# Top-32 attention and a gated mixture: seven column parts, a bound used in place, and another mask on GpSimd

## The chip, the cores and the metric

The kernel runs on one core of a Trainium2 chip. Its time is the device time of one execution in microseconds (us). The kernel before took 844.89 us, the median of three runs (844.6 to 846.16).

## What is computed

Eight batches with eight heads each, 576 tokens, 64 values a head. For every row of scores only the 32 largest count:

```python
scores = scale * np.matmul(q, k.transpose(0, 1, 3, 2))
kth = np.partition(scores, -top_k, axis=-1)[..., -top_k:-top_k + 1]
scores = np.where(scores >= kth, scores, -1000000000.0)
attn = softmax(scores)          # over the row
x = attn @ v                    # heads side by side: 8 x 576 x 512
```

Then, in each batch, the 128 tokens with the largest `x @ w_gate` get `sigmoid(gate) * relu(x @ w1) @ w2` added (w1 is 512 x 1024). This document calls that the mixture.

## The kernel before, in words

**Units.** The attention is cut into 144 units, 18 a batch. A unit holds two rows of heads for 128 queries: a tile `sc` of 128 partitions x 2 heads x 576 scores. The loop at line 1083 goes over n; in one turn it works on several units at once, each at another stage. Every instruction is recorded by the helper at line 43 and kept in program order on its engine, so the order of the code is the order of each queue; the trace shows nearly all instructions under L43, and they are told apart by their tiles.

**The stages of a unit**, by engine:

1. TensorE multiplies the scores (`multiply`, line 352); ScalarE copies them from PSUM to `sc` (`keep`, 369). This is done one turn ahead.
2. VectorE looks for a bound near the 24th largest (`find_bound`, 383). MAX8 gives the eight largest of each of eight parts of 72 columns. Three rounds of MAX8 on the candidates (the best 3, 7, 8 of each part), with MATCH_REPLACE8 between, give `best[2]`, whose eighth value is the bound.
3. One turn later ScalarE (`cut`, 413) casts the upper half of the bound's float32 to `seen`, then takes Sign of bound less score (`part`, 420), with the sum of the signs, which counts how many scores lie above. GpSimd multiplies score and sign (`y`) and appends eight filling values that depend on the count (`fill`, 435).
4. Another turn later VectorE takes the eight largest of `y`'s 584 columns (`find_kth`, 444): the eighth is the 32nd largest of the row.
5. Another turn later the mask `less` is made (`mask`, 449): of the unit's two heads, ScalarE makes one, as Relu(32nd - score), and GpSimd the other, as the comparison score < 32nd, 1 or 0. In the 9 units where GpSimd is not used, VectorE makes it.
6. Another turn later TensorE transposes the scores in 128 x 128 pieces (`turn_some`, 476) and adds `less` times a diagonal matrix of -2^90 (`out_of_reach`) into the same PSUM piece. Eight pieces lie in the tile `ptr`. The ninth, the last 64 columns of one head beside those of the other, lies in `av` (`turn_last`, 498). ScalarE then takes the exponential (`pT`, `last`), TensorE multiplies with `v` (`values`, 510), and ScalarE copies the result to `xs`.

**Other work in the turns.** `weigh` (1043) is followed by the next unit's mask, the scores of unit n+1, none, one or two transposes of the next batch's rows (`loads_at`), the products of `values`, and one step of an earlier batch's mixture (`mix_at`: products with w1 and w2). The first mixture step on TensorE falls some 33 units in. In the first units of each batch there are turns with no row transposes or no mixture step.

**The end.** After the last unit the last batch's mixture runs by itself. A set of checks (`seen`, `sums`, ranks) is reduced on VectorE to one number; if it says that a row's count was outside what the method can handle, a general path (`general`, 1315) computes everything again.

**What orders TensorE's array.** The products have different shapes: 128 rows x 128 columns for transposes and mask products, 64 x 128 for the scores (64 values a head), 128 x 64 for the products with v.

Of the kernel before, what the change touches and what calls it, by code (L numbers as in the profile page):

```python
# [11 lines left out]
ALU = mybir.AluOpType  # L12
FP32 = mybir.dt.float32
BF16 = mybir.dt.bfloat16
I32 = mybir.dt.int32
# [6 lines left out]
BIG = 2.0**90  # L22
# [4 lines left out]
LEAST = 1.0e-16 * SMALLER  # L27
# [2 lines left out]


J = 4


class InOrder:
# [11 lines left out]
def kernel(  # L47
# [28 lines left out]
    const = ctx.enter_context(tc.tile_pool(name="const", bufs=1))  # L76
# [3 lines left out]
    wkpool = ctx.enter_context(tc.tile_pool(name="wk", bufs=2))  # L80
    stats = ctx.enter_context(tc.tile_pool(name="stats", bufs=6))
# [38 lines left out]
    nc.vector.tensor_copy(out=slot, in_=slot_i)  # L120


    out_of_reach = const.tile([P, P], BF16, name="out_of_reach")
    nc.vector.tensor_scalar_mul(out_of_reach, ident, -BIG)

    NS = B * 2 * (J * NHP + NHP // 2)
    seen = const.tile([P, 3, NS], FP32, name="seen")  # L130
    sums = const.tile([P, B * NT, H], FP32, name="sums")
    nc.gpsimd.memset(sums, 1.0)

    MIDDLE = S - 2 * (TOP_K - 8) + 1
# [30 lines left out]
    def load_weights():  # L165
# [169 lines left out]
    def groups(t):  # L335

        return NHP // 2 if t == J else NHP
# [42 lines left out]
            )  # L380
        return sc

    def find_bound(sc):

        w = S // 8
        cand = wkpool.tile([P, 2, 64], FP32, name="cand")
        best = [stats.tile([P, 2, 8], FP32, name=f"best{r}") for r in range(3)]  # L390
        for i in range(2):

            if i == 1:
                flush_vector()
            for u in range(8):
                dve.max(cand[:, i, 8 * u : 8 * u + 8], sc[:, i, u * w : (u + 1) * w])


        parts = cand.rearrange("p i (u e) -> p i u e", u=8)
# [11 lines left out]
        return best[2]  # L411

    def cut(best, at):

        act.copy(
            out=seen[:, 0, at : at + 2],
            in_=best.rearrange("p i e -> p (i e)").bitcast(BF16)[:, 15:32:16],
        )

    def part(i, sc, at, sides):  # L420

        act.activation(
            sides[:, i, :],
            sc[:, i, :],
            AF.Sign,
            bias=seen[:, 0, at + i : at + i + 1],  # L430
            scale=-(1.0 + 2.0**-23),
            accum_out=seen[:, 2, at + i : at + i + 1],
        )

    def fill(y, at):

        pool.tensor_tensor(
            y[:, :, S : S + 8],
            steps,
            seen[:, 2, at : at + 2].unsqueeze(2).to_broadcast([P, 2, 8]),  # L440
            ALU.subtract,
        )

# [5 lines left out]
    def mask(sc, next8, on=None):  # L449

        less = wkpool.tile([P, 2, S], BF16, name="less")
        for i, engine in enumerate(on or (act, pool)):
            kth = next8[:, i, 7:8]
            if engine is act:
                act.activation(less[:, i, :], sc[:, i, :], AF.Relu, bias=kth, scale=-1.0)
            else:

                def is_less(engine=engine, i=i, kth=kth):
                    (engine or dve).tensor_scalar(
                        out=less[:, i, :],
                        in0=sc[:, i, :],
                        scalar1=kth,
                        scalar2=None,
                        op0=ALU.is_lt,
                    )

                if engine:  # L470
                    is_less()
                else:
                    vector_late.insert(0, is_less)
        return less

    def turn_some(tr, z, less):

        pe.transpose(tr, z, ident)
        if less is not None:
            pe.matmul(  # L480
                tr, less, out_of_reach, start=False, stop=True, skip_group_check=True
            )

    def room_to_turn():
        return ps_tr.tile([P, 2, J, P], FP32, name="ptr"), ps_av.tile(
# [3 lines left out]
    def turn(z, tr, less=None):  # L489

        for i in range(2):
            for c in range(J):
                at = slice(c * P + i * R, (c + 1) * P + i * R)
                turn_some(
                    tr[:, i, c, :], z[:, i, at], None if less is None else less[:, i, at]
                )

    def turn_last(z, av, less=None):

        tr = av[:, 512 - P : 512]
        last = [
            a and a.rearrange("p i s -> p (i s)")[:, JP : JP + P] for a in (z, less)
        ]
        turn_some(tr, *last)
        return tr

    def values(t, g, pT, last, av, vs):  # L510
# [475 lines left out]
    per_batch = sum(groups(t) for t in range(NT))  # L986
# [27 lines left out]
    for b in range(B - 1):  # L1014
        n = (b + 1) * per_batch + mix_at_of.get(b, mix_at)[6]
# [11 lines left out]
    def warm_up():  # L1027
        ps = ps_av.tile([P, 512], FP32, name="av")
        for _ in range(48):
            pe.matmul(ps[:, 0:P], out_of_reach, out_of_reach)  # L1030

    warm_up()
    turn_pair(first_rows, 0, dve.tensor_copy)
# [1 line left out]
    loading = iter(())  # L1035
    inverting = normalised = None
    of_batch = {}
    scs, bests, ys, next8s, masks = {}, {}, {}, {}, {}

    def is_unit(n):  # L1040
        return 0 <= n < N
# [1 line left out]
    def weigh(sc, tr, av, less):  # L1043
# [9 lines left out]

        return pT, last, exp

    def what_is_below(n):
        at, sc = 2 * n, scs[n]
        cut(bests.pop(n), at)
        sides = wkpool.tile([P, 2, S], BF16, name="sides")
        y = wkpool.tile([P, 2, S + 8], FP32, name="y")  # L1060
        for i in range(2):
            part(i, sc, at, sides)
            pool.tensor_tensor(y[:, i, 0:S], sc[:, i, :], sides[:, i, :], ALU.mult)
        fill(y, at)
        ys[n] = y

    def kth_of(n):
# [2 lines left out]
            next8s[b] = stats.tile([P, per_batch, 2, 8], FP32, name="next8", bufs=2)  # L1070
        find_kth(ys.pop(n), next8s[b][:, i, :, :])

    def mask_of(n, on=None):
        b, i = divmod(n, per_batch)
        masks[n] = mask(scs[n], next8s[b][:, i, :, :], on)
        if i == per_batch - 1:
            at = 2 * per_batch * b
            pool.tensor_copy(
                out=seen[:, 1, at : at + 2 * per_batch].rearrange("p (n i) -> p n i", i=2),
                in_=next8s.pop(b)[:, :, :, 7],  # L1080
            )

    for n in range(-1, N):
        b, i = divmod(n, per_batch)
# [63 lines left out]


        if is_unit(n):  # L1150
            bests[n] = find_bound(scs[n])
        flush_vector()
        flush_pool()
        if is_unit(n - 2):
# [8 lines left out]
        if gating is not None:  # L1163
            b, t = gating
# [5 lines left out]
        b, i = divmod(n, per_batch)  # L1170
# [69 lines left out]
    next(closed)  # L1240


    sure = stats.tile([P, 1], FP32, name="sure")
    dve.memset(sure, 1.0)
    for what, op, than, limit in (
        (seen[:, 0, :], ALU.min, ALU.is_gt, LEAST),
        (seen[:, 1, :], ALU.min, ALU.is_gt, LEAST),
        (seen[:, 2, :], ALU.max, ALU.is_lt, float(MIDDLE)),
        (seen[:, 2, :], ALU.min, ALU.is_gt, float(MIDDLE - 16)),
        (sums.rearrange("p t h -> p (t h)"), ALU.min, ALU.is_gt, FEWEST),  # L1250
        (sums.rearrange("p t h -> p (t h)"), ALU.max, ALU.is_lt, MOST),
    ):
# [138 lines left out]
```

## Time and profile before

| | us |
|---|---|
| median of 3 runs | 844.89 |
| profiled execution | 845.82 |
| its span, first to last instruction | 844.0 |
| TensorE (PE) busy | 793.1 |
| VectorE (DVE) busy | 805.4 |
| ScalarE (ACT) busy | 759.5 |
| GpSimd (POOL) busy | 729.6 |

A group's line in the profile has the engine, the operation, the tile written and those read, the shape out and in, the number of instructions, their busy time in us, the mean duration of one in ns, and the idle time ahead of them with what ended it. PE is TensorE's products, PEld its weight loads. An engine's next instruction may begin before the one ahead has ended, so the cost of one in a row of equals is the distance between starts, which is less than its duration. TensorE's ends are modelled. The granted TensorE clock was 0.992 on average.

### The profile page before, as it was taken

What the parts mean: (1) busy time and instruction counts of PE and PEld (TensorE: products, weight loads), DVE (VectorE), ACT (ScalarE), POOL (GpSimd) and SP (SyncE); (2) the same over time, 40 slices, a digit from 0 to 9 for tenths busy, and PEclk for the clock granted to TensorE, in tenths of its full rate; (3) what the DMA queues carried; (4) which work ended last, traced back from release to release, by engine and by line L of the source; (5) the groups of instructions that cost most, each with busy time, mean ns of one, the idle gap of its engine ahead of it and who ended that gap; (6) DMA issues with size and microseconds to landing.
All of it is one profiled execution on the core that took longest, in us unless ns stands there. A gap on an engine that the chain in (4) does not pass through costs nothing. (4 is left out here: it accounts for less than half of the span.)

```text
span 844.0 us, 28167 instructions
## 1 busy us (share of the span) xinstructions
PE 793.1 (94%) x9887; PEld 612.4 (73%) x9887; DVE 805.4 (95%) x4905; ACT 759.5 (90%) x1701; POOL 729.6 (86%) x730
## 2 busy tenths in 40 slices
PE   6898888998999999999999999999999999999987
PEld 5666666666787778877787777877788777867754
DVE  7899999999999999999999999999999999999960
ACT  4799999999999999999999999999999999979831
POOL 3689889989989899999999999999999999989831
PEclk9699999999999999999999999999999999999999
DMA  8931111411141221511323221412215102101021
GB/s 171 279 75 29 40 64 26 104 45 35 58 97 28 52 40 58 110 40 27 89 37 82 51 47 56 101 30 52 39 58 110 27 2 76 23 2 27 2 70 30
DMA packets 122134, 50.38 MB, mean 60 GB/s; under 512 B 116416, under 2 KB 116416, under 8 KB 120960
## 3 DMA queue, kind: packets, MB, share of 16 engines
q1 hardware_dynamic: 118672, 43.91, 21.6%
q0 software_dynamic: 1728, 4.20, 2.8%
q8 instruction: 80, 1.31, 0.7%
q14 instruction: 70, 0.57, 0.3%
q10 hardware_dynamic: 1584, 0.39, 0.2%
HBM read 36.93 MB, written 11.55 MB: 57 GB/s over the span
## 5 line engine op out<-in xcount | busy, mean ns | idle before, releaser
L43 POOL TENSOR_TENSOR y<-sc,sides 128x576 f32<-128x576 f32 x288 | 365.0, 1288 | 73.1 <-ACT sides L43 70.0
L43 DVE MAX8 cand<-sc 128x8 f32<-128x72 f32 x2304 | 330.9, 218 | 1.7 <-ACT sc L43 1.7
L43 POOL TENSOR_SCALAR less<-sc,next 128x576 bf16<-128x576 f32 x135 | 232.9, 1725 | 3.2 <-DVE next L43 2.5
L43 ACT ACTIVATE sides<-sc,seen 128x576 bf16<-128x576 f32 x288 | 221.0, 768 | 5.2
L43 PE MATMUL ptr<-out_of_reach,less 128*128 128x128 bf16 x1136 | 204.8, 220 | 16.2 <-POOL less L43 16.0
L43 PE MATMUL ptr<-ident,sc 128*128 128x128 f32 x1136 | 214.4, 279 | 0.0
L43 DVE MAX8 next<-y 128x8 f32<-128x584 f32 x288 | 204.4, 751 | 3.2 <-POOL y L43 3.2
L43 PE MATMUL ps<-kT,qT 64*128 64x288 f32 (+1 forms) x1280 | 180.9, 431 | 7.6 <-ACT qT L43 5.8
L43 PEld LDWEIGHTS av<-v,pT 128*64 128x64 f32 x4544 | 144.1, 137 | 46.3 <-ACT last L43 33.7
L43 PEld LDWEIGHTS ptr<-ident,sc 128*128 128x128 f32 x1136 | 160.8, 142 | 22.4 <-PE av L43 8.7
L43 PE MATMUL av<-v,pT 128*64 128x65 f32 x4544 | 163.7, 224 | 13.8 <-ACT last L43 12.2
L43 ACT COPY sc<-ps 128x1152 f32<-128x1152 f32 (+1 forms) x144 | 160.5, 1114 | 8.5 <-PE ps L43 7.2
L43 ACT ACTIVATE pT<-ptr 128x1024 f32<-128x1024 f32 x142 | 144.1, 1015 | 18.1 <-PE ptr L43 14.6
L43 PEld LDWEIGHTS <-less 128*128 128x128 bf16 x1296 | 133.2, 104 | 36.4 <-POOL less L43 21.8
L43 DVE MAX8 best<-cand 128x8 f32<-128x24 f32 (+2 forms) x864 | 142.4, 201 | 0.1
L43 PEld LDWEIGHTS ps<-kT,qT 64*128 64x128 f32 (+1 forms) x1280 | 97.8, 177 | 46.6 <-issue 22.1
L43 ACT ACTIVATE less<-sc,next 128x576 bf16<-128x576 f32 x143 | 110.6, 774 | 6.5 <-DVE next L43 6.3
L43 DVE MATCH_REPLACE8 cand<-best,cand 128x24 f32<-128x24 f32 (+1 forms) x576 | 101.9, 185 | 0.0
L43 PE MATMUL av<-vpair,last 128*128 128x130 f32 (+1 forms) x314 | 68.1, 317 | 0.0
L43 PE MATMUL h_ps<-xeT,w 128*128 128x128 f32 x464 | 61.6, 277 | 0.0
L43 PEld LDWEIGHTS h_ps<-xeT,w 128*128 128x128 f32 x464 | 56.0, 192 | 2.1 <-issue 1.2
L43 PE MATMUL y_ps<-w,hT 128*128 128x512 f32 x112 | 56.7, 601 | 0.0
(129 smaller groups left out, 869.7 us busy)
## 6 DMA issues: line engine op xcount, KB each, us to landing
v<-in_v_dram SPq DMA_DIRECT2D x64, 128.0 KB, 3.3
out_dram<-x SPq DMA_DIRECT2D x8, 1024.0 KB, 4.1
rows<-in_k_dram SPq DMA_DIRECT2D x56, 128.0 KB, 2.9
rows<-in_q_dram SPq DMA_DIRECT2D x56, 128.0 KB, 3.1
w<-in_moe_w_dram SPq DMA_DIRECT2D x2, 2048.0 KB
gate_row<-row_dram SPq DMA_DIRECT2D x7, 288.0 KB, 5.1
w<-in_k_dram SPq DMA_DIRECT2D x8, 128.0 KB, 3.4
last<-in_k_dram SPq DMA_DIRECT2D x8, 128.0 KB, 3.5
```

The lines of the kernel that those rows point to most:

```text
L43: return lambda *a, **kw: self._tc.keep_in_program_order(fn(*a, **kw))
```

## The change

It does four things.

1. `find_bound` cuts the 576 columns into 7 parts of 82 or 83 and not 8 of 72.
2. The bound is used in place: the third round writes into a tile `bound` that holds a batch's bounds, and Sign reads it there. `cut` and its cast are gone. What the checks need of the bounds and of the 32nd values is reduced on VectorE once a batch (`keep_least`, new), and no longer copied to `seen` (by GpSimd once a batch, for the 32nd).
3. GpSimd's mask (and VectorE's, where it stands in) for the unit's second head is min(score - 32nd, 0). It is at most 0, so it is multiplied by +2^90; `out_of_reach` becomes two matrices.
4. The ninth mask product holds columns of both heads, which now need different signs: it becomes two products of 64 columns each.

```diff
-    def find_bound(sc):
-        w = S // 8
-        cand = wkpool.tile([P, 2, 64], FP32, name="cand")
-        best = [stats.tile([P, 2, 8], FP32, name=f"best{r}") for r in range(3)]
+    def find_bound(sc, bound):
+        cand = wkpool.tile([P, 2, 8 * PARTS], FP32, name="cand")
+        best = [stats.tile([P, 2, 8], FP32, name=f"best{r}") for r in range(2)]
+        best.append(bound)
...
-            for u in range(8):
-                dve.max(cand[:, i, 8 * u : 8 * u + 8], sc[:, i, u * w : (u + 1) * w])
+            for u in range(PARTS):
+                dve.max(
+                    cand[:, i, 8 * u : 8 * u + 8],
+                    sc[:, i, u * S // PARTS : (u + 1) * S // PARTS],
+                )
...
-    def cut(best, at):
-        act.copy(
-            out=seen[:, 0, at : at + 2],
-            in_=best.rearrange("p i e -> p (i e)").bitcast(BF16)[:, 15:32:16],
-        )
...
-            bias=seen[:, 0, at + i : at + i + 1],
+            bias=bound[:, i, 7:8],
...
                         scalar1=kth,
-                        scalar2=None,
-                        op0=ALU.is_lt,
+                        scalar2=0.0 if i else None,
+                        op0=ALU.subtract if i else ALU.is_lt,
+                        **(dict(op1=ALU.min) if i else {}),
...
-    def turn_some(tr, z, less):
+    def turn_some(tr, z, less, heads):
         pe.transpose(tr, z, ident)
         if less is not None:
-            pe.matmul(
-                tr, less, out_of_reach, start=False, stop=True, skip_group_check=True
-            )
+            n = P // len(heads)
+            for u, i in enumerate(heads):
+                pe.matmul(
+                    tr[u * n : (u + 1) * n],
+                    less[:, u * n : (u + 1) * n],
+                    out_of_reach[i],
+                    start=False,
+                    stop=True,
+                    skip_group_check=True,
+                )
...
+    def keep_least(b, bound, kth):
+        low = stats.tile([P, per_batch, 2], I32, name="low", bufs=1)
+        dve.tensor_scalar(
+            out=low,
+            in0=bound.bitcast(I32),
+            scalar1=(1 << 23) - 1,
+            scalar2=1,
+            op0=ALU.bitwise_and,
+            op1=ALU.bitwise_xor,
+        )
+        for w, of in enumerate((bound, kth, low)):
+            dve.tensor_reduce(
+                out=least[:, w, b : b + 1], in_=of, axis=mybir.AxisListType.XY, op=ALU.min
+            )
```

`turn` passes one head to `turn_some`, `turn_last` both. The last batch's `keep_least` stands among the checks at the end, which read `least` (three reductions of 8) in place of two of `seen`'s 288 columns.

More of the change, by code (lines that the diff above doesn't have):

```diff
@@ L32 @@
 J = 4
+PARTS = 7
 class InOrder:
@@ L120 @@
     nc.vector.tensor_copy(out=slot, in_=slot_i)
-    out_of_reach = const.tile([P, P], BF16, name="out_of_reach")
-    nc.vector.tensor_scalar_mul(out_of_reach, ident, -BIG)
+    out_of_reach = [const.tile([P, P], BF16, name=f"out_of_reach{i}") for i in range(2)]
+    for i in range(2):
+        nc.vector.tensor_scalar_mul(out_of_reach[i], ident, BIG if i else -BIG)
     NS = B * 2 * (J * NHP + NHP // 2)
-    seen = const.tile([P, 3, NS], FP32, name="seen")
+    seen = const.tile([P, NS], FP32, name="seen")
+    least = const.tile([P, 3, B], FP32, name="least")
     sums = const.tile([P, B * NT, H], FP32, name="sums")
@@ L394, in find_bound @@
                 flush_vector()
-            for u in range(8):
-                dve.max(cand[:, i, 8 * u : 8 * u + 8], sc[:, i, u * w : (u + 1) * w])
-        parts = cand.rearrange("p i (u e) -> p i u e", u=8)
+            for u in range(PARTS):
[3 more added lines that the diff above has]
+                )
+        parts = cand.rearrange("p i (u e) -> p i u e", u=PARTS)
         for r, e in enumerate((3, 7, 8)):
@@ L410, in find_bound, with part @@
                     )
-        return best[2]
-    def cut(best, at):
-        act.copy(
-            out=seen[:, 0, at : at + 2],
-            in_=best.rearrange("p i e -> p (i e)").bitcast(BF16)[:, 15:32:16],
-        )
-    def part(i, sc, at, sides):
+    def part(i, sc, bound, at, sides):
         act.activation(
@@ L429, in part @@
             AF.Sign,
-            bias=seen[:, 0, at + i : at + i + 1],
+            bias=bound[:, i, 7:8],
             scale=-(1.0 + 2.0**-23),
-            accum_out=seen[:, 2, at + i : at + i + 1],
+            accum_out=seen[:, at + i : at + i + 1],
         )
@@ L439, in fill @@
             steps,
-            seen[:, 2, at : at + 2].unsqueeze(2).to_broadcast([P, 2, 8]),
+            seen[:, at : at + 2].unsqueeze(2).to_broadcast([P, 2, 8]),
             ALU.subtract,
@@ L494, in turn @@
                 turn_some(
-                    tr[:, i, c, :], z[:, i, at], None if less is None else less[:, i, at]
+                    tr[:, i, c, :],
+                    z[:, i, at],
+                    None if less is None else less[:, i, at],
+                    [i],
                 )
@@ L506, in turn_last @@
         ]
-        turn_some(tr, *last)
+        turn_some(tr, *last, range(2))
         return tr
@@ L1029, in warm_up @@
         for _ in range(48):
-            pe.matmul(ps[:, 0:P], out_of_reach, out_of_reach)
+            pe.matmul(ps[:, 0:P], out_of_reach[0], out_of_reach[0])
     warm_up()
@@ L1037 @@
     of_batch = {}
-    scs, bests, ys, next8s, masks = {}, {}, {}, {}, {}
+    scs, bounds, ys, next8s, masks = {}, {}, {}, {}, {}
     def is_unit(n):
@@ L1054, in weigh, with bound_of @@
         return pT, last, exp
+    def bound_of(n):
+        b, i = divmod(n, per_batch)
+        if i == 0:
+            bounds[b] = stats.tile([P, per_batch, 2, 8], FP32, name="bound", bufs=2)
+        find_bound(scs[n], bounds[b][:, i, :, :])
     def what_is_below(n):
         at, sc = 2 * n, scs[n]
-        cut(bests.pop(n), at)
+        b, i = divmod(n, per_batch)
+        bound = bounds[b][:, i, :, :]
         sides = wkpool.tile([P, 2, S], BF16, name="sides")
@@ L1061, in what_is_below @@
         for i in range(2):
-            part(i, sc, at, sides)
+            part(i, sc, bound, at, sides)
             pool.tensor_tensor(y[:, i, 0:S], sc[:, i, :], sides[:, i, :], ALU.mult)
@@ L1075, in mask_of @@
         masks[n] = mask(scs[n], next8s[b][:, i, :, :], on)
[L1076 to L1081, printed above, removed]
+        if i == per_batch - 1 and b < B - 1:
+            keep_least(b, bounds.pop(b)[:, :, :, 7], next8s.pop(b)[:, :, :, 7])
     for n in range(-1, N):
@@ L1150 @@
         if is_unit(n):
-            bests[n] = find_bound(scs[n])
+            bound_of(n)
         flush_vector()
@@ L1240 @@
     next(closed)
+    keep_least(B - 1, bounds.pop(B - 1)[:, :, :, 7], next8s.pop(B - 1)[:, :, :, 7])
     sure = stats.tile([P, 1], FP32, name="sure")
@@ L1245 @@
     for what, op, than, limit in (
[L1246 to L1249, printed above, removed]
+        (least[:, 0, :], ALU.min, ALU.is_gt, LEAST),
+        (least[:, 1, :], ALU.min, ALU.is_gt, LEAST),
+        (least[:, 2, :], ALU.min, ALU.is_gt, 0.5),
+        (seen, ALU.max, ALU.is_lt, float(MIDDLE)),
+        (seen, ALU.min, ALU.is_gt, float(MIDDLE - 16)),
         (sums.rearrange("p t h -> p (t h)"), ALU.min, ALU.is_gt, FEWEST),
```

## Prediction

> **What bounds the kernel now.** I read the page's engine shares first, then busy time stretch by stretch, then the timeline of single units. The page's shares (PE 94%, DVE 95%, ACT 90%, POOL 86%) name no bound, so the second view cuts the span at unit boundaries: units before any mixture step (28 to 205.8 us), the head of one batch (two units and a bit), its other 15 units, the last batch, the tail. Columns: stretch and its length, then busy us of PE, PEld, DVE, ACT, POOL.
>
> ```profile
> 28.00:205.80 177.80, 159.25 (x2099) 120.82 (x2097) 175.13 (x1077) 168.56 (x378) 160.96 (x153) 0.98 0.29 75
> ...
> 399.40:415.50 16.10, 14.76 (x201) 12.02 (x200) 16.10 (x103) 15.73 (x36) 14.40 (x14) 1.00 0.28 51
> 415.50:498.00 82.50, 82.35 (x1032) 63.43 (x1031) 82.39 (x508) 79.45 (x180) 76.49 (x76) 1.00 0.26 60
> ...
> 695.40:796.40 101.00, 98.15 (x1253) 78.64 (x1252) 99.68 (x623) 91.75 (x203) 92.46 (x91) 1.00 0.12 27
> ```
>
> Before the mixtures VectorE is the bound (175.13 of 177.80 us) and TensorE idles 18.55 us. Afterwards two engines are full at once: in 15 units of a batch TensorE works 82.35 of 82.50 us and VectorE 82.39. All that TensorE waits in a batch of 98.6 us is 1.34 us at its head and 0.15 us in the rest. So what VectorE saves is worth its full price for the first third of 144 units, and afterwards at most 1.49 us a batch; and whatever TensorE is given extra is then paid. That "busy" TensorE is really full I take from its starts: they repeat to 0.01 us from unit to unit in those 15 units.
>
> The third view is TensorE's timeline at the end of one unit's turning (start, length, instruction). What counts is the distance between starts, since the ends are modelled.
>
> ```profile
> 405.11 0.22 PE L43 MATMUL ptr<-out_of_reach,less 128*128 128x128 bf16 x1
> 405.16 0.28 PE L43 MATMUL ptr<-ident,sc 128*128 128x128 f32 x1
> 405.28 0.22 PE L43 MATMUL ptr<-out_of_reach,less 128*128 128x128 bf16 x1
> 405.33 0.28 PE L43 MATMUL av<-ident,sc 128*128 128x128 f32 x1
> 405.45 0.22 PE L43 MATMUL av<-out_of_reach,less 128*128 128x128 bf16 x1
> 405.60 1.24 PE L43 MATMUL ps<-kT,qT 64*128 64x288 f32 x8
> ```
>
> A mask product holds TensorE 0.05 us when another 128*128 product follows (405.11 to 405.16), but 0.15 us when the scores follow, which use the array as 64*128 (405.45 to 405.60). The change of tile shape costs about 0.095 us.
>
> **VectorE's saving.** A unit has 16 MAX8 of 72 columns, whose starts stand 134 ns apart; the two MAX8 of 584 columns stand 668 ns apart. That is (668-134)/512 = 1.04 ns a column and 59 ns fixed. Seven parts of 82 or 83 columns make 14 x (59 + 82.3 x 1.04) = 2.03 us against 16 x 134 = 2.14: 0.118 us less. The merge shrinks from 24, 56 and 64 candidates to 21, 49 and 56: for two heads 2 x (3+7+8) columns of MAX8 and 2 x (3+7) of MATCH_REPLACE8, 56 x 1.04 = 0.058 us. Together 0.176 us a unit.
>
> keep_least adds four small instructions a batch. A reduction of 288 columns took 446 ns, so one of 36 about 446 - 252 x 1.04 = 184 ns; three of these and one elementwise instruction, 0.7 us a batch.
>
> In the first stretch 33 units pass; from about the sixth VectorE is behind the scores, so 30 units x 0.176 - 0.7 = **-4.6 us**. What is late next there: ScalarE, 168.56/33 = 5.11 us a unit, less the cast; POOL 4.88; VectorE stays the bound at about 5.2.
>
> **ScalarE.** One cast a unit goes (203 ns mean, off the path by VectorE and TensorE). It matters twice: at the head of a batch, where TensorE's 1.34 us are waits for ScalarE's exponentials and ScalarE is 15.73 of 16.10 us busy, and in the tail, where the last unit's cast stands between VectorE's bound and Sign (**-0.2 us**).
>
> **TensorE's extra.** One product a unit, the ninth mask product (av<-out_of_reach,less), is split into two of 64 columns. The shape becomes 128*64, so a change of shape is added in front of it; the one behind it, to the scores, is there already. Price by rows: the second of two rows' transposes to the first 128*64 product is 0.20 us from start to start, against 0.11 between products of one shape, so 0.092. The two halves lie in different columns of the array; 32 products of av<-v,pT, in that form, take 1.15 us, two side by side, the second 7 ns after the first. So 0.092 + 0.007 = 0.099 us a unit. From both sides: 0.007 (no change of shape paid) to 0.2 (paid twice, or halves one after another). I take 0.099, since all four changes of shape in a unit show 0.092 to 0.097.
>
> A page speaks for more: by the Trainium skill, TensorEngine Tiling (Array Packing), section Restrictions, column tiling switches the fast weight load off. The trace has 104 ns for the bf16 load of 128 columns and 137 ns for a float32 load of 64; no run here shows a bf16 load of 64. If it were 137, each unit would pay 0.033 us more, and the sum would end 3.5 us higher.
>
> In a mixture batch: 18 x 0.099 = 1.78 us more work, against 1.49 us of waits. VectorE now has 18 x 0.176 - 0.7 = 2.5 us to spare a batch, so the mask comes earlier, ScalarE saves 3 x 0.2 at the head, and I let 0.3 us of waits remain: 1.78 - 1.19 = +0.6 a batch, **+3.0 us** over the five from 205.8 to 695.4. In the last batch TensorE waits 2.85 us; 1.2 of that I leave, for its mixture steps are crowded: 1.78 - 1.65 = **+0.1 us**. TensorE is the bound from there on.
>
> **GpSimd's mask.** The trace has no subtract-and-min.
>
> ```profile
> L43 POOL TENSOR_SCALAR less<-sc,next 128x576 bf16<-128x576 f32 x135 | 232.9, 1725 | 3.2 <-DVE next L43 2.5 <-DVE place L43 0.5 <-POOL y L43 0.2
> ...
> L43 POOL TENSOR_SCALAR pick<-slot,ranks 128x128 bf16<-128x128 f32 x21 | 12.8, 611 | 0.9 <-DVE junk L43 0.9
> ...
> L43 POOL TENSOR_SCALAR pick<-slot,ranks,others 128x128 bf16<-128x128 f32 x3 | 2.4, 806 | 0.0
> ```
>
> These are one comparison of 576, one of 128, and a subtraction with a comparison of 128. The comparison costs (1725-611)/448 = 2.49 ns a column; the subtraction added 195 ns to 128 columns. Above: if all of that grows with the width and min costs what the comparison did, 1725 + 4.5 x 195 = 2.6 us. Below: GpSimd's cheapest row, a memset of 2080 columns in 1841 ns, 0.89 ns a column, gives 0.7 us. I take 1.7 to 1.9, nearest to the row it replaces. It is worth nothing either way while POOL isn't the bound: it works 76.49 of 82.50 us in full units, 5.1 of 5.5 each, so the mask may grow by 0.4 us to 2.1. A shorter mask gains nothing where TensorE or VectorE is the bound.
>
> The Trainium skill, GPSIMD Engine Reference, section Elementwise — side-by-side cycle accounting, has bodies of up to two operations at 1.03 cycles an element at 1.2 GHz, which would make some 0.8 us of the new mask by estimate. The comparison's 2.49 ns is three such cycles, so this firmware is not at that rate. By the page the second rival below falls away; the forecast stays.
>
> **Rest.** The copy of the eighth values to seen leaves POOL (8 x 239 ns, hidden). At the end the checks get about 0.4 us longer on VectorE; their product on TensorE (823.26 us) is covered by the copy of xeT until 824.01, so nothing, and 0.4 us if that cover were gone. No DMA moves.
>
> **Sum.** -4.6 + 3.0 + 0.1 - 0.2 = -1.7 us. The profiled execution took 845.82 us (span 844.0), so 844.1; that run lay 0.9 us above the median of 844.89, and on the median the forecast is **843.2 us**.
>
> **Rivals.**
> 1. Slower: TensorE's waits stay. If they come from the length of the exponentials and not from late masks, TensorE keeps its 1.49 and 2.85 us and pays all the extra: 6 x 1.78 = +10.7, -4.6 - 0.2: 850.8. Against it: in other units without a row transpose the wait is under 0.1 us. It decides from 0.64 us of waits left per batch. Chance 0.14.
> 2. Slower: POOL becomes the bound. At 2.3 us a mask POOL needs 4.88 + 0.57 = 5.45 us a unit in the first stretch (5.39 now) and 5.64 later (5.48 now): 33 x 0.06 + 107 x 0.16 = +19 us, 864. It decides from about 2.2 us; beyond, each 0.1 us costs 13 us (135 masks). Chance 0.13.
> 3. The split pays no change of shape: 0.092 x 107 units = -9.8 from the forecast, 833.4. Chance 0.07. Against it, every change of shape in the trace is paid.
> 4. The split costs 0.2 us: +10.8, 854. Chance 0.05.
> 5. It doesn't do what it says: seven parts make it likelier that one part holds more than eight of the best 24, and the guard (24 to 31 values above the bound in every row) sends the kernel through the general path, far longer than any range. Counted on the reference's inputs, the largest is 31, in one row of 36,864. Chance 0.01.
>
> **How the numbers follow.** The forecast has 0.60, with a spread of its own of 840 to 846, from 0.05 to 0.6 us of waits left. 0.2% is 1.7 us, about what a measurement tells from no change; the forecast lies at that edge. Faster: 0.37 of the forecast's 0.60 and rival 3, 0.44. Same: 0.21 of it. Slower: its last 0.02 and rivals 1, 2, 4 and 5, 0.35. The range 838 to 855 takes in rivals 1 and 4 and the beginning of rival 2 (a mask of 2.2 us); it leaves out the rest of rival 2, and rivals 3 and 5, together 0.2.
>
> **What would show it.** After: MAX8 of cand 2016 times, 145 ns apart; VectorE with idle time (some 2.5 us a batch) after 206 us, TensorE over 99% busy there; the first mixture unit about 4.6 us earlier; 0.2 us from the last transpose to the first half of the mask product, 0.15 from the second to the scores; POOL's mask row under 2.1 us. It is wrong if POOL is full, if VectorE stays full after 206 us, or if a batch is shorter than 98.6 us.

## The result, and the profile after

The changed kernel took **866.71 us** (median of four runs, 864.12 to 868.57), the kernel before in the same comparison 845.25: a ratio of 1.0251, 95% interval 1.0218 to 1.0284. The prediction was 843.2 with a range of 838 to 855. The profiled execution took 864.12 us (span 861.8) at the same granted clock as before, 0.992.

The same view that carried the prediction, stretch by stretch: units before the first mixture step, the head of one batch, its other units, the last batch. Columns: stretch and length, busy us of PE, PEld, DVE, ACT, POOL, then clock, DMA share, GB/s.

```profile
26.40:209.50 183.10, 162.22 (x2128) 123.41 (x2127) 176.90 (x1016) 166.32 (x345) 176.41 (x152) 0.98 0.29 74
407.00:423.50 16.50, 15.36 (x205) 12.32 (x204) 16.50 (x79) 15.38 (x34) 15.99 (x14) 1.00 0.26 49
423.50:507.90 84.40, 84.22 (x1046) 64.84 (x1045) 83.96 (x499) 77.48 (x164) 82.45 (x75) 1.00 0.27 59
709.90:814.50 104.60, 100.76 (x1271) 80.38 (x1270) 102.31 (x582) 88.63 (x186) 99.39 (x90) 1.00 0.12 26
```

Each of these stretches is longer, the first by 5.3 us although VectorE was given less to do. The column that has changed is the last: GpSimd worked 160.96 of 177.80 us in the first stretch and now 176.41 of 183.10; in the units of a batch it has gone from 76.49 of 82.50 to 82.45 of 84.40. A fourth engine is nearly full.

The costliest groups, each shape by itself: busy us, mean ns of one, then the idle time ahead of them and what ended it.

```profile
L45 POOL TENSOR_SCALAR less<-sc,next 128x576 bf16<-128x576 f32 x135 | 303.1, 2245 | 2.6 <-DVE next L45 1.2 <-PE ps L45 0.5 <-DVE place L45 0.4
...
L45 PE MATMUL ptr<-out_of_reach,less 128*128 128x128 bf16 x1136 | 206.4, 220 | 30.0 <-POOL less L45 29.4
...
L45 PEld LDWEIGHTS <-less 128*64 128x64 bf16 x288 | 15.8, 106 | 17.5 <-issue 0.2
```

GpSimd's mask takes 2245 ns, where the comparison took 1725. And TensorE's idle time ahead of its mask products, ended by GpSimd's `less`, is 29.4 us. Before it was 16.0:

```profile
L43 PE MATMUL ptr<-out_of_reach,less 128*128 128x128 bf16 x1136 | 204.8, 220 | 16.2 <-POOL less L43 16.0
```

TensorE's timeline in one batch of the changed kernel shows the place (start, length, instruction, idle time ahead and its releaser):

```profile
413.33 0.28 PE L45 MATMUL av<-ident,sc 128*128 128x128 f32 x1
413.54 0.25 PE L45 MATMUL av<-out_of_reach,less 128*64 128x128 bf16 x2
413.72 1.24 PE L45 MATMUL ps<-kT,qT 64*128 64x288 f32 x8
...
417.88 0.28 PE L45 MATMUL ptr<-ident,sc 128*128 128x128 f32 x1
419.06 0.23 PE L45 MATMUL ptr<-out_of_reach,less 128*128 128x128 bf16 x1 [0.89 <-POOL less L45]
```

The first three lines are the split product: 0.21 us from the transpose to the first half and 0.18 to the scores, 0.39, where before it was 0.12 and 0.15. So the split costs 0.12 us a unit, not 0.099. The last two are the first product of GpSimd's head: a transpose stands in the array, and the mask to be added comes 1.1 us late (1.18 us from start to start, where the four pairs ahead of it have 0.11 or 0.12).

### The profile page after: what moved, and what is told of

Its sections match the earlier page's. It is cut to its first block, busy times and chain, and to the rows that moved or that the text cites. A ratio compares the mean times of both kernels' runs of the same rounds, so it can differ in the third digit from the quotient of the medians.

```text
span 861.8 us, 28053 instructions
## 1 busy us (share of the span) xinstructions
PE 809.7 (94%) x10031; PEld 624.4 (72%) x10031; DVE 816.7 (95%) x4652; ACT 741.5 (86%) x1557; POOL 789.7 (92%) x722
## 3 DMA queue, kind: packets, MB, share of 16 engines
q8 instruction: 81, 1.33, 0.7%
## 5 line engine op out<-in xcount | busy, mean ns | idle before, releaser
L45 POOL TENSOR_TENSOR y<-sc,sides 128x576 f32<-128x576 f32 x288 | 373.6, 1331 | 30.9 <-ACT sides L45 29.2
L45 DVE MAX8 cand<-sc 128x8 f32<-128x82 f32 (+1 forms) x2016 | 313.9, 227 | 1.4 <-ACT sc L45 1.3
L45 POOL TENSOR_SCALAR less<-sc,next 128x576 bf16<-128x576 f32 x135 | 303.1, 2245 | 2.6 <-DVE next L45 1.2
L45 PE MATMUL ptr<-out_of_reach,less 128*128 128x128 bf16 x1136 | 206.4, 220 | 30.0 <-POOL less L45 29.4
L45 ACT ACTIVATE sides<-sc,bound 128x576 bf16<-128x576 f32 x288 | 221.0, 773 | 0.0
L45 PE MATMUL ptr<-ident,sc 128*128 128x128 f32 x1136 | 217.1, 280 | 0.0
L45 PEld LDWEIGHTS <-less 128*128 128x128 bf16 (+1 forms) x1440 | 134.0, 104 | 70.3 <-POOL less L45 38.9
L45 DVE MATCH_REPLACE8 cand<-best,cand 128x21 f32<-128x21 f32 (+1 forms) x576 | 98.9, 179 | 0.0
L45 DVE MAX8 best<-cand 128x8 f32<-128x21 f32 (+1 forms) x576 | 90.2, 189 | 0.0
L45 DVE CUSTOM_DVE_ANT_0 prod<-x,wg 128x512 f32<-128x512 f32 (+1 forms) x40 | 54.5, 1361 | 5.3 <-POOL x L45 5.2
```

The lines of the kernel that those rows point to most:

```text
L45: return lambda *a, **kw: self._tc.keep_in_program_order(fn(*a, **kw))
```

## The experiments

Effects are given as differences of ratios to the kernel before, times 845 us. That kernel had medians of 845.72, 844.17 and 846.71 us in the three groups of runs. "Both" in the table stands for seven parts and the bound in place, "long mask" for the subtraction with min.

| kernel | median us | ratio, 95% interval |
|---|---|---|
| seven parts alone | 842.18 | 0.9973, 0.9957 to 0.999 |
| bound in place alone | 839.79 | 0.9918, 0.9896 to 0.994 |
| both, old mask | 835.84 | 0.9900, 0.9874 to 0.9926 |
| both, + 8 columns on GpSimd | 838.10 | 0.9909, 0.9881 to 0.9938 |
| both, + 80 columns behind the mask | 849.36 | 1.0048, 1.003 to 1.0066 |
| both, + 80 columns ahead of the mask | 855.30 | 1.0100, 1.0076 to 1.0123 |
| both, long mask, no split | 859.46 | 1.0176, 1.0151 to 1.02 |
| the same, VectorE relieved | 862.27 | 1.0204, 1.017 to 1.0237 |
| the change | 866.71 | 1.0251, 1.0218 to 1.0284 |
| split alone | 853.56 | 1.0098, 1.0072 to 1.0123 |
| long mask and split alone | 876.52 | 1.0368, 1.0344 to 1.0392 |

### Four kernels that take the change apart

**Seven parts and bound in place, with the old mask** (no split).

```diff
-                        op0=ALU.subtract if i else ALU.is_lt,
-                        **(dict(op1=ALU.min) if i else {}),
+                        op0=ALU.is_lt,
```

> The changed kernel with the comparison as GpSimd's mask again and so with one ninth mask product: seven parts and the bound used in place, alone. Theory 1 (the long mask does the harm: it fills GpSimd, and VectorE's instructions with two inputs or of the copying kind wait for it; the split adds 0.125 us a unit on TensorE): both gone, so POOL's mask is 1.72 us again, the first mixture unit comes about 4.6 us earlier than before, a mixture batch takes 97.3 to 98.6 us, and the kernel takes 832 to 841 us. Theory 2 (the seven parts or the bound's reductions do the harm on VectorE): over 850 us, and the VectorE rows of prod and less are as long as in the changed kernel (1294 and 2140 ns from start to start).

**The long mask and the split alone**, on the kernel before.

```diff
-                        op0=ALU.is_lt,
+                        op0=ALU.subtract if i else ALU.is_lt,
+                        **(dict(op1=ALU.min) if i else {}),
```

> The kernel before with subtract-and-min as GpSimd's mask, and with the ninth product in two halves that this needs; eight parts and the cast stay. Theory 1: VectorE has its old work and the longer waits for GpSimd on top, 14 us in prod and 10 in its own masks; 870 to 885 us, slower than the changed kernel. Theory 2: 853 to 860 us, faster than the changed kernel, only the split being paid.

**The split alone**, on the kernel before: both halves with -2^90.

```diff
-            pe.matmul(
-                tr, less, out_of_reach, start=False, stop=True, skip_group_check=True
-            )
+            n = P // len(heads)
+            for u, i in enumerate(heads):
+                pe.matmul(tr[u * n : (u + 1) * n], less[:, u * n : (u + 1) * n], out_of_reach[i],
+                          start=False, stop=True, skip_group_check=True)
```

> The kernel before with the ninth mask product in two halves, both with the same matrix; all else as before. It prices the split alone. By the changed kernel's starts (0.209 us from the ninth transpose to the first half against 0.115, 0.173 from the last half to the scores against 0.149) it is 0.125 us a unit or 2.25 us a mixture batch. If TensorE's waits at the head of a batch stay, all of it is paid: 6 x 2.25, 857 to 860 us. If they take it up, 848 to 852 us.

**The long mask without the split**: the changed kernel with max in place of min, and with one ninth product as before. Its second head has the larger scores masked.

```diff
-                        **(dict(op1=ALU.min) if i else {}),
+                        **(dict(op1=ALU.max) if i else {}),
```

> The changed kernel with max in place of min on GpSimd, so that the mask has the sign of ScalarE's and one ninth product does; it then masks the larger scores of the second head, so its output is not the reference's. It has the long mask without the split. Theory 1 (mask and split both cost): the stretch before the mixtures is as long as in the changed kernel (183 us against 177.3 before), the mixture batches lose the split's 2.25 us; 848 to 854 us. If the split alone does the harm: 832 to 842 us. If the mask alone: 864 to 868 us.

Measured: parts and bound -8.5 us; the split +8.3 alone, +6.3 on top of the rest; the long mask +23.3 on top of parts and bound, +22.8 on top of the split alone. Each step measured on the kernel before, or on the split alone, they add up to -8.5 + 8.3 + 22.8 = 22.6, against 21.2 for the whole change, which is within their uncertainty of some 3 us each. Two runs fell between their expectations: the split alone (853.56, expected 848 to 852 or 857 to 860) and the long mask without it (859.46, expected 848 to 854 or, with the mask alone to blame, 864 to 868). **The long mask is the loss**, and without it and its split the rest of the change beats both kernels. Of the kernel with both and the old mask, then of the one with the long mask and no split, the two rows that moved:

```profile
L45 POOL TENSOR_SCALAR less<-sc,next 128x576 bf16<-128x576 f32 x135 | 232.9, 1725 | 3.8 <-DVE next L45 2.9 <-DVE place L45 0.6 <-POOL y L45 0.2
...
L45 PE MATMUL ptr<-out_of_reach,less 128*128 128x128 bf16 x1136 | 204.9, 220 | 14.8 <-POOL less L45 14.5
```

```profile
L45 POOL TENSOR_SCALAR less<-sc,next 128x576 bf16<-128x576 f32 x135 | 303.2, 2246 | 2.3 <-DVE next L45 1.4 <-DVE place L45 0.3
...
L45 PE MATMUL ptr<-out_of_reach,less 128*128 128x128 bf16 x1136 | 207.0, 220 | 36.2 <-POOL less L45 34.7
```

TensorE's wait for GpSimd's mask goes from 14.5 to 34.7 us, 20.2 us more, where the time grew by 23.3.

### Why 0.5 us a unit costs so much

Two theories stood. Theory 1: GpSimd is full. Theory 2: some instructions of VectorE take longer in the changed kernel (its own ten masks 1947 ns, before 931; the product of `x` and `w_gate`, `prod`, 1361, before 1012), because they wait for the GpSimd instruction that runs, and a longer one makes longer waits.

**The load without the length**, in the kernel with both and the old mask.

```diff
                     is_less()
+                    if engine is pool:
+                        pool.tensor_scalar(out=spare, in0=sc[:, i, 0:80], scalar1=kth,
+                                           scalar2=None, op0=ALU.is_lt)
```

> The seven parts and the bound in place with the old comparison mask (835.84 us), and after each of GpSimd's masks a second comparison of 80 columns into a spare tile that nobody reads, some 0.49 us by its rows: GpSimd gets the load of the new mask, about 0.5 us a unit, but no single instruction of it becomes longer. Theory 1 (GpSimd is full): the time rises as with the long mask, to 856 to 860 us, and GpSimd's idle time in units 10 to 32 falls from 7.9 to about 3 us. Theory 2 (VectorE's two-input instructions wait for the GpSimd instruction that is running, and a longer one makes longer waits): only the load is added, the longest instruction is the old one, so the time stays at 838 to 845 us, and the product of the guard on VectorE (prod) stays at 6.8 to 8 us in units 10 to 32.

**VectorE relieved**, in the kernel with both and the long mask without the split.

```diff
-        for w, of in enumerate((bound, kth, low)):
+        for w, of in enumerate((bound, kth)):
...
-            mask_of(n - 3, (act, None) if n in scatter_steps else None)
+            mask_of(n - 3, (act, act) if n in scatter_steps else None)
```

> The seven parts, the bound in place and the subtracting mask with max for min and one ninth product (859.46 us; it masks the larger scores, so its output is not the reference's), and now without the elementwise check of the bounds (low) and with ScalarE making both masks in the nine units in which VectorE made one. VectorE loses some 3.9 us of busy time a batch, most of it waiting for GpSimd; ScalarE gets two masks of 0.7 us in the steps in question. Theory 1 (GpSimd is full): a batch stays at 100 us, the time at 855 to 860 us. Theory 2 (VectorE's waits for GpSimd): a batch falls to 98 to 98.5 us, the time to 846 to 850 us.

The extra load came out between its two expectations: +12.5 us, more than half of the long mask's loss by load alone. The relieved kernel took 862.27 us, above both of its expectations. It relieved VectorE less than meant: its busy time fell by 4.4 us in all and not by 3.9 a batch. Six of its ten masks went to ScalarE, the four of the last three units stayed; and where a mask had gone, the wait came back in `prod`, whose eight 64-row instructions took 3160 ns, before that 1332. Still VectorE stands idle some 3 us in two batches, where it had been full, and a batch is 100.7 us, not 98. That speaks against theory 2 without settling it (ScalarE's two masks may have eaten a part). Theory 2 needs its mechanism, too, and that was measured next.

**Prices at the end of the kernel** with both and the old mask.

```diff
+    price(pool, half[:, 0, :], ALU.is_lt)
+    price(pool, half[:, 0, :], ALU.subtract)
+    price(pool, half[:, 0, :], ALU.subtract, ALU.min)
+    price(pool, half[:, 0, :], ALU.min)
...
+    dve.max(best8, full[:, 0, 0:S])
+    price(pool, full[:, 1, 0:S], ALU.subtract, ALU.min)
+    price(dve, half[:, 1, :], ALU.subtract, ALU.min)
```

> The kernel with seven parts, bound in place and the comparison mask, and behind its end a row of instructions on 576 float32 columns that compute nothing that is read: GpSimd alone, one after another, with a comparison, a subtraction, a subtraction with min and a min alone, into bf16 and into float32; then VectorE's MAX8, one-input and two-input instructions each started beside a running subtraction with min on GpSimd. Expected of GpSimd: comparison 1.72 us, subtraction with min 2.2 us into bf16. If the second operation is what costs, subtraction alone and min alone stay near 1.7 us; if it is min, or the subtraction, that one is near 2.2 us by itself. If the float32 output matters, the float32 rows differ from the bf16 rows. Of VectorE: theory 2 has its mask or its product last until GpSimd's instruction has ended (about 2 us and not 0.5 to 0.7), while MAX8 is not held up.

GpSimd's timeline: subtraction, subtraction with min, min (bf16 out); comparison, subtraction with min (float32 out).

```profile
817.50 1.72 POOL L45 TENSOR_SCALAR sides<-w,wg 128x576 bf16<-128x576 f32 x1
819.31 2.22 POOL L45 TENSOR_SCALAR sides<-w,wg 128x576 bf16<-128x576 f32 x1
821.62 1.73 POOL L45 TENSOR_SCALAR sides<-w,wg 128x576 bf16<-128x576 f32 x1
823.33 1.73 POOL L45 TENSOR_SCALAR y<-w,wg 128x576 f32<-128x576 f32 x1
825.15 2.22 POOL L45 TENSOR_SCALAR y<-w,wg 128x576 f32<-128x576 f32 x1
```

Comparison, subtraction and min all cost 1.72 to 1.73 us; subtraction with min, two operations in one instruction, costs 0.49 us more, and the output's type nothing. (The comparison into bf16 ran beside the end of an indirect DMA and took 2.31.) VectorE's timeline in the same kernel, its mask started inside GpSimd's subtraction with min (829.16 to 831.37):

```profile
829.22 0.76 DVE L45 MAX8 best<-y 128x8 f32<-128x576 f32 x1 [14.95 <-POOL y L45]
829.89 0.50 DVE L45 TENSOR_SCALAR sides<-w,wg 128x576 bf16<-128x576 f32 x1
```

0.50 us: GpSimd's long mask doesn't hold VectorE's mask up. `prod` wasn't tried so, but one in the run with the long mask and no split shows the same: it ran from 235.93 to 238.22 us, beyond GpSimd's multiplies, which ended at 236.79, and it ended inside GpSimd's long mask, which ran from 236.94 to 239.14. Theory 2 falls in the form it had. What does hold it up is seen in the unit masks that VectorE makes. The timeline of before, then of after: VectorE's mask and GpSimd's multiplies beside it (before, the second of its pair; after, both in one line).

```profile
402.28 1.29 POOL L43 TENSOR_TENSOR y<-sc,sides 128x576 f32<-128x576 f32 x1
...
402.82 1.08 DVE L43 TENSOR_SCALAR less<-sc,next 128x576 bf16<-128x576 f32 x1
```

```profile
409.16 2.94 DVE L45 TENSOR_SCALAR less<-sc,next 128x576 bf16<-128x576 f32 x1
...
409.26 2.52 POOL L45 TENSOR_TENSOR y<-sc,sides 128x576 f32<-128x576 f32 x2
```

Each time VectorE's mask ends 0.3 us after the pair of multiplies has ended (403.57 and 403.90; 411.78 and 412.10). Before it began in the second of the pair, after 0.10 us ahead of the first: where GpSimd stands when VectorE arrives sets the wait, and a late GpSimd puts both multiplies in front. That VectorE's waits are a consequence here is a reading; the run with the extra load fits it, where VectorE's masks went from 1000 to 1169 ns though no instruction of GpSimd's had been made longer.

**That wait by itself**, at the end of the same kernel.

```diff
+    dve.max(best8, full[:, 0, 0:S])
+    multiply2(pool, full[:, 1, 0:S])
+    multiply2(pool, full[:, 1, 0:S])
+    price(dve, half[:, 1, :], ALU.subtract, ALU.min)
```

> The kernel with seven parts, bound in place and the comparison mask, and behind its end instructions on 576 float32 columns whose results nobody reads: a multiply of two tensors on GpSimd alone; then two such multiplies with VectorE's subtraction with min started inside the first; then that VectorE instruction beside GpSimd's subtraction with min; then VectorE's own multiply beside GpSimd's; then VectorE's subtraction with min alone. By the rows of the unit masks VectorE's instruction ends 0.33 us after GpSimd's multiplies have ended, however many stand in a row: expected 0.50 us alone and beside GpSimd's mask, and about 2.2 us inside two multiplies. If VectorE waits only for the one that runs, about 1 us.

VectorE's mask beside a multiply, beside GpSimd's subtraction with min, then VectorE's multiply beside GpSimd's, and the mask alone:

```profile
817.00 0.98 DVE L45 TENSOR_SCALAR sides<-w,wg 128x576 bf16<-128x576 f32 x1
...
819.95 0.50 DVE L45 TENSOR_SCALAR sides<-w,wg 128x576 bf16<-128x576 f32 x1
...
822.26 1.16 DVE L45 TENSOR_TENSOR y<-w 128x576 f32<-128x576 f32 x1
...
824.02 0.49 DVE L45 TENSOR_SCALAR sides<-w,wg 128x576 bf16<-128x576 f32 x1
```

The 2.2 us expected inside two multiplies didn't come: 0.98, until 0.33 us after the one that ran (which ended at 817.65). Here the next multiply started 0.08 us behind it; in the kernel the two of a pair overlap by 0.05. That VectorE takes the gap is a reading, not tried by itself.

### Load, lateness, and where it begins to cost

**The extra comparison ahead of the mask**, in the kernel with both and the old mask.

```diff
+                    if engine is pool:
+                        pool.tensor_scalar(out=spare, in0=sc[:, i, 0:80], scalar1=kth,
+                                           scalar2=None, op0=ALU.is_lt)
                     is_less()
```

> As the run with the 80-column comparison behind each of GpSimd's masks (849.36 us), with that comparison ahead of the mask instead of behind it: the same load on GpSimd, but each mask ends 0.5 us later in its own unit, as the long mask does. Of the long mask's 23.6 us the load alone made 13.5; open is the rest. Theory 3 (the rest is the mask's own lateness: TensorE stands at its first mask product): 857 to 861 us, and the waits at ptr<-out_of_reach,less in a batch as with the long mask (2.6 to 2.8 us). Theory 4 (the rest comes of the length of one instruction, through VectorE's and GpSimd's waits for one another): 848 to 851 us.

**Half the load**, behind the mask.

```diff
-    spare = const.tile([P, 80], BF16, name="spare")
+    spare = const.tile([P, 8], BF16, name="spare")
```

> As that run with the comparison behind the mask, but of 8 columns in place of 80, some 0.24 us by the row of 16 columns: half the load. The prediction had GpSimd's load free up to about 0.4 us a unit: then the time is that without it, 835 to 838 us. If GpSimd's backlog at the head of a batch counts from the first tenth of a microsecond on, the time lies between, near 842 us.

With half the load (0.28 us a unit from start to start) the time is that without it, +0.8 us and inside the intervals. With 0.46 us it is +12.5, and with the mask late by that as well +16.9. The rows of the run behind the mask, then ahead of it:

```profile
L45 PE MATMUL ptr<-out_of_reach,less 128*128 128x128 bf16 x1136 | 206.1, 220 | 26.2 <-POOL less L45 25.0
...
L45 POOL TENSOR_SCALAR spare<-sc,next 128x80 bf16<-128x80 f32 x135 | 68.8, 510 | 0.0
```

```profile
L45 PE MATMUL ptr<-out_of_reach,less 128*128 128x128 bf16 x1136 | 206.5, 221 | 32.5 <-POOL less L45 31.7
```

25.0, 31.7 and, with the long mask, 34.7 us: the same wait grows each time. So somewhere between 0.28 and 0.46 us a unit GpSimd becomes the bound. Where it begins differs by stretch: with 0.28 us a batch was no longer in the profiled executions (97.8 us against 98.0), but units 10 to 32 took 122.95 us against 120.74. In those units GpSimd had 0.35 us a unit idle without the load (it worked 112.78 us), in a batch 0.41 (90.73 of 98.04).

Load makes some 12.5 us of the loss, and the lateness of the mask in its own unit 4.4. The rest, 6.4 us by the ratios (each difference uncertain by about 3 us) and 2.2 by the profiled spans (854.0 and 856.2), stays open. Part of it can be load again: the long mask adds 0.49 us a unit and not 0.46, and 135 x 0.03 is 4 us by estimate, if GpSimd is the bound throughout. Neither expectation for the run ahead of the mask, 857 to 861 or 848 to 851, held it.

### Which half of the gain is whose

**Seven parts alone**, on the kernel before, and **the bound in place alone**, on the changed kernel with the old mask and one ninth product:

```diff
-            for u in range(8):
-                dve.max(cand[:, i, 8 * u : 8 * u + 8], sc[:, i, u * w : (u + 1) * w])
+            for u in range(PARTS):
...
```

> The kernel before with seven parts in place of eight and nothing else changed: ScalarE still casts the bound, the mask is the comparison. With the bound in place as well it took 835.84 us against 845.72. If VectorE's work is what counts in the first stretch, as the prediction has it, nearly all of the 9.9 us is there: 836 to 839 us, with the first stretch about 5 us shorter. If the cast on ScalarE, between VectorE's bound and the count, is what holds the units back (latency, and ScalarE's exponentials at the head of a batch), most of the gain is absent: 841 to 845 us.

```diff
-PARTS = 7
+PARTS = 8
```

> The bound used in place, with eight parts as before and the comparison mask: the other half of what took 835.84 us. Seven parts alone made 842.18 against 844.17. If the two effects add up, this run is at 0.9925 to 0.995 of the kernel before, 838 to 840 us, with the first ten units some 3 us shorter and each batch some 0.5 us shorter: the cast on ScalarE, which the prediction costed at nothing outside the tail and the head of a batch, is then the larger gain. If they don't add up (each alone uncovers the other's engine), it stays within 1.7 us of the kernel before.

Seven parts -2.3 us, the bound in place -6.9, both -8.5. The first fell where it was expected if the cast counts (841 to 845): VectorE's shorter search alone is worth little. The second was inside its 838 to 840. The profiled executions, in us, the first stretch from the first unit's turning to the first mixture unit's (units 0 to 32), a batch as the mean of two:

| kernel | units 0 to 32 | clock in units 0 to 9 | units 10 to 32 | a batch |
|---|---|---|---|---|
| before | 177.27 | 0.95 | 123.18 | 98.7 |
| seven parts | 176.53 | 0.94 | 122.06 | 98.6 |
| bound in place | 174.78 | 0.93 | 121.81 | 98.1 |
| both | 171.75 | 0.98 | 120.74 | 98.0 |

The execution with both was granted a higher clock in its first ten units than the others, so its first column can't be set beside theirs: 3.1 of its 5.5 us fall there. From unit 10 on all four were granted 1.00, and the effects add: -1.1, -1.4 and -2.4.

## Why the prediction was wrong

**GpSimd's mask: the step that failed.** It took the new mask at 1.7 to 1.9 us as "nearest to the row it replaces". The nearest row was the other one: the subtraction with a comparison is also an instruction of two operations, and 195 ns dearer on 128 columns. If that had been a fixed cost, the mask had been 1.92 us, if it grew with the width, 2.6. Both lie above what was taken. Measured, alone: 2.22 us, in the kernel 2.245, and the second operation costs (490 - 195)/448 = 0.66 ns a column. (The lower bound of 0.7 us was off too: 576 columns at 0.89 ns are 0.5.)

The Trainium skill, GPSIMD Engine Reference, section Elementwise — side-by-side cycle accounting, has 1.03 cycles an element for bodies of up to two operations. At 1.2 GHz, and with the comparison's fixed 0.29 us (1725 ns less 576 x 2.49), both masks would be at some 0.8 us by estimate; 1.72 and 2.22 differ from it in the rate and in the second operation, which isn't free here.

**"POOL may grow to 2.1 us", and rival 2's threshold of 2.2.** Rival 2 named the mechanism. That its 864 us lies near the 866.71 is chance: its own sum, with the 2.245 us that the mask took, gives some 857, and it holds nothing of the split. Its threshold was worked out with unit lengths of the kernel before (5.39 us, 5.48), while the same text made the units of the changed kernel shorter. Against its own forecast of 5.2 us in the first stretch the room was 5.2 - 4.88 = 0.3 us, and the runs show a bound between 0.28 and 0.46. The reckoning with the lengths that hold, from the stretches of the kernel with both and the old mask (GpSimd worked 160.13 of 171.80 us, and 90.73 of a batch's 98.0): 160.13 + 33 x 0.49 = 176.3, that is 4.5 us over; 90.73 + 17 x 0.49 = 99.1, 1.1 over. Over the first stretch and six batches that is some 11 us, half of the 23.3 that the long mask cost. Most of the rest is what GpSimd didn't fill: with the long mask it worked 124.19 of 127.02 us in units 10 to 32 and 98.42 of 100.05 in a batch, so 0.12 and 0.09 us a unit stayed idle.

**"I let 0.3 us of waits remain" at a batch's head.** Most of them remain, which was rival 1. TensorE's timeline at a head before, then in the kernel with seven parts and the bound in place:

```profile
407.71 1.15 PE L43 MATMUL av<-v,pT 128*64 128x65 f32 x32 [0.63 <-ACT last L43]
...
413.21 1.16 PE L43 MATMUL av<-v,pT 128*64 128x65 f32 x32 [0.70 <-ACT last L43]
```

```profile
398.76 1.15 PE L45 MATMUL av<-v,pT 128*64 128x65 f32 x32 [0.50 <-ACT last L45]
...
403.98 1.15 PE L45 MATMUL av<-v,pT 128*64 128x65 f32 x32 [0.43 <-ACT last L45]
```

These are waits for ScalarE's exponential of the ninth piece, 0.93 us, before 1.33. With seven parts alone they are 0.65 and 0.71, with the bound in place alone 0.39 and 0.43: what shortened them came with the bound in place and not with VectorE's spare time. Of the split they take up little: with it alone on the kernel before, 0.40 and 0.59 us are left.

**The cast "off the path by VectorE and TensorE".** Using the bound in place is the larger gain, 6.9 us, so something of it was on the path; that it is the cast, and not the smaller copies that went with it, is likely but not tried by itself. In the first stretch the two cuts together give -5.5 us, near the -4.6 forecast, but that is luck: 3.1 of it fall in the ten units with the higher clock. From unit 10 on seven parts give 1.1 us, where the forecast had 23 x 0.176 = 4.0 us less work on VectorE; its busy time fell by 2.1 (123.07 to 120.98), and 1.1 us of idle time came up. A reading that fits: VectorE's search and ScalarE's cast lie in one chain, bound, cast, sign, multiply, 32nd value, and a busy share of 175.13 in 177.80 us, in which VectorE's waits for GpSimd count as work, didn't say that VectorE alone was that chain.

**The split: 0.099 us.** Measured 0.12, inside its bounds. By the Trainium skill, TensorEngine Tiling (Array Packing), section Restrictions, column tiling switches the fast weight load off. The 137 ns that the prediction feared for it didn't come: 106 ns for 64 columns, against 104 for 128. That half the columns took as long doesn't speak against the page. The split alone costs 8.3 us, where 18 x 0.12 in six batches would be 13: some of it passes inside the head's waits, as forecast, but less than 1.19 us a batch; a batch is 1.6 us longer.

**What held.** The full units of TensorE pay what they are given; what the prediction named as its refutation, a POOL that is full and a VectorE that stays full after 206 us, is what refuted it.

## What to carry to other kernels

Price an operation that the trace lacks from a row with the same number of operations, not from the one it replaces, and let that row's fixed part be the lowest price. An engine that isn't the bound has as much room as the *new* length of the unit leaves it, less about a tenth of a microsecond a unit here that it can't fill; when two engines get faster, the room of a third shrinks. Effects that are measured by stretch need the same granted clock in that stretch. A change with several edits is worth taking apart on the chip: here two of four made the kernel 1% faster, and the other two took it and 2.5% more.

## What the runs showed of the hardware

VectorE's mask, an instruction with one tensor read, waits while GpSimd multiplies two tensors (0.98 to 2.94 us, ended 0.3 us after the multiply), but not beside GpSimd's mask (0.50, alone 0.49); MAX8 beside either takes 0.76, and 0.75 alone. A VectorE multiply of two tensors took 1.16 us beside GpSimd's multiply. It took 0.76 when it began in the last 0.27 us of one GpSimd mask, and the next mask, which began beside it, took 2.47 instead of 2.21. So GpSimd seems to pay as well, and one engine's length in a trace depends on what the other does in the same microsecond.

The Trainium skill, SBUF — State Buffer, section SBUF: two separate sides, has the pair of ports that VectorE and GpSimd share as an exclusive lock, held by whichever starts first for its whole instruction; on VectorE's side it names instructions in a two-port mode or with two inputs in SBUF. The waits behind multiplies that were already running agree with it, if VectorE's mask is in such a mode, which no run here shows by itself. Two rows don't fit: VectorE's mask at 0.50 us inside GpSimd's mask of 2.21, and the one that began at 409.16, 0.10 us ahead of GpSimd's multiplies by the recorded starts, and waited for both. So which instruction GpSimd runs counts here too; that it is the number of tensors read is one reading.
